# A new order for the first key tile, and the clamp in phi moved to GpSimd

One core of one Trainium2 chip. The metric is device time of one execution in microseconds (us), the median of several runs.

## The reference, cut to what matters

Two branches on the same `x` (2048 rows of 512, bf16), mixed by a gate of each row:

```python
qkv = x @ wqkv                                              # attention branch, 32 heads of 16
phi = lambda t: where(t > 0, t + 1, exp(t)) + 1e-6
kv  = einsum("bhsd,bhse->bhde", phi(k), v); z = sum(phi(k), over s)
o   = (phi(q) @ kv) / (phi(q) . z) ;  a = o @ wo
b   = gelu(layernorm(x).T @ w1 + b1) @ w2 + b2, transposed   # token branch
out = g * a + (1 - g) * b,  g = sigmoid(sum(x * gate_w))
```

phi is computed as max(t, 0) + (min(exp(t), 1) + 1e-6). The clamp of the title is the second bracket. phi runs 32 times on tiles of 128 partitions x 512 columns: 16 of keys, then 16 of queries.

## The kernel before

There are four stages. The *key stage* turns each x tile into keys, phi of the keys, and a 512 x 512 product `gacc` of x and phi(k). The *query stage* runs the first `uacc` matmuls of the token branch between the query matmuls. The rest of the `uacc` matmuls and the output stage (`aps`, `yps`) come last. Each engine runs its own instructions in program order (VectorE before: the copy of tile 2 at 6.24 us, its statistics at 6.58, the clamp at 7.60). In the names, kacc2 stands for the key matmuls of x tile 2, xT for a transposed x tile, e for its exp and pk (pqT for queries) for its phi. The parts that matter:

```python
def phi(dst, acc):                            # acc: PSUM bank of a key or query tile
    e = work.tile([P, SC], BF16, ...)
    nc.scalar.activation(out=e, in_=acc, func=Exp)                       # ScalarE
    nc.vector.tensor_scalar(out=e, in0=e, 1.0, 1e-6, min, add)           # VectorE: the clamp
    nc.vector.scalar_tensor_tensor(out=dst, in0=acc, 0.0, in1=e, max, add)   # VectorE: "combine", S(t)

def ln_step(u):                               # statistics of x tile u for the layer norm
    bn_stats, bn_aggr                                                    # VectorE
    if u % 4 == 3:                            # every fourth tile
        nc.vector.tensor_scalar_add(veps, ...)                           # VectorE
        nc.gpsimd.tensor_tensor(rstd, veps, -0.5, pow)                   # GpSimd
...
transpose_tile(0); transpose_tile(1)          # TensorE, then a copy by VectorE and one by ScalarE
for t in range(2): k_part(t, range(2))        # first two of four key matmuls
transpose_tile(2)
ln_step(0)
for t in range(3):
    k_part(t, rest); k_phi(t)
ln_step(1)
for t in range(3, 16):
    k_part(t); k_phi(t)                       # 4 key matmuls, phi
    if t >= 4: g_tile(t - 4)                  # 4 gacc matmuls of the tile 4 back
    if t >  4: ln_step(t - 3)                 # so rstd falls at t = 6, 10, 14
    if t == 6: load_small()                   # three small loads issued by GpSimd
    if t >= 9: ln_apply(t - 9)                # ScalarE: normalise, needs nmr (VectorE, from rstd)
    if t % 4 == 0 and t >= 8: ln_shift(...)   # VectorE: nmr
```

Tiles from 3 on reach TensorE already transposed, by DMA.

Of the kernel before, what the change touches and what calls it, by code (L numbers as in the profile page):

```python
# [7 lines left out]
ACT = mybir.ActivationFunctionType  # L8
# [7 lines left out]
def kernel(  # L16
# [13 lines left out]
    nc = tc.nc  # L30
    P = nc.NUM_PARTITIONS
# [9 lines left out]
    ND = D // P  # L41
# [25 lines left out]
    def keep(shape, dtype, name):  # L67
        return persist.tile(shape, dtype, name=name, tag=name)

    def bank(name, dtype=FP32):  # L70
        return ps.tile([P, SC], dtype, name=name, tag="bank")

    xs = keep([P, NT, D], BF16, "xs")
    hs = keep([P, NT, D], BF16, "hs")
    xT = keep([P, ND, S], BF16, "xT")
# [17 lines left out]
    ident = keep([P, P], BF16, "ident")  # L93
# [18 lines left out]
    def mm(o, lhsT, rhs, start, stop, **kw):  # L112
        nc.tensor.matmul(o, lhsT=lhsT, rhs=rhs, start=start, stop=stop, **kw)  # L113
# [20 lines left out]
    def load_xT(t0, n):  # L134
# [14 lines left out]
        out=ident[:], in_=ident[:], compare_op=ALU.not_equal, fill=1.0, base=0,  # L149
# [5 lines left out]
        out=maskQ[:], in_=maskH[:].rearrange("p (a m) -> p m a", m=2), op=ALU.max, axis=AX.X  # L155
# [4 lines left out]
        out=xT[:, :, 3 * P : 3 * P + 2],  # L160
        in_=xs[:, 0, 0 : 2 * ND].rearrange("p (k c) -> p k c", k=ND),
# [10 lines left out]
    for c, (j0, nb) in enumerate(w1_chunks):  # L172
        w = wpool.tile([P, NT, FB * P], BF16, name="w1c", tag="wc")
        w1c.append(w)
        for t0 in range(0, NT, 8) if c < 3 else (0,):
            t1 = t0 + 8 if c < 3 else NT
            nc.sync.dma_start(
                out=w[:, t0:t1, : nb * P], in_=w1_view[:, t0:t1, j0 * P : (j0 + nb) * P]
# [15 lines left out]
    def warm_up(n, cols=SC):  # L194
        for _ in range(n):
            mm(wps[:, :cols], warm[:, 0:P], warm[:, :cols], True, True)
# [2 lines left out]
    nc.scalar.activation(out=act_warm[:], in_=ones_f[:], func=ACT.Exp)  # L199
    warm_up(6)  # L200

    def transpose_tile(t):
        pt = bank("pt")
        for k in range(ND):
            mm(pt[:, k * P : (k + 1) * P], xs[:, t, k * P : (k + 1) * P], ident[:], True, True)
        H = ND // 2
        src = pt[:].rearrange("p (k s) -> p k s", k=ND)
        dst = xT[:, :, t * P : (t + 1) * P]
        nc.vector.tensor_copy(out=dst[:, 0:H], in_=src[:, 0:H])  # L209
        nc.scalar.activation(out=dst[:, H:], in_=src[:, H:], func=ACT.Copy)  # L210

    def phi(dst, acc):
        e = work.tile([P, SC], BF16, name="e", tag="e", bufs=6)
        nc.scalar.activation(out=e[:], in_=acc[:], func=ACT.Exp)  # L214
        nc.vector.tensor_scalar(  # L215
            out=e[:], in0=e[:], scalar1=1.0, scalar2=PHI_EPS, op0=ALU.min, op1=ALU.add
        )
        nc.vector.scalar_tensor_tensor(  # L218
            out=dst, in0=acc[:], scalar=0.0, in1=e[:], op0=ALU.max, op1=ALU.add
        )  # L220
# [3 lines left out]
    def k_part(t, ks):  # L224
        if t not in kaccs:
            kaccs[t] = bank("kacc")
        for k in ks:
            mm(
                kaccs[t][:], xT[:, k, t * P : (t + 1) * P], wk_sb[:, k, :],
                k == 0, k == ND - 1,  # L230
            )

    def k_phi(t):
        phi(pk[:, t, :], kaccs.pop(t))
# [32 lines left out]
    def q_block(i):  # L267
        c, j = divmod(i, ND)
        qacc = bank("qacc")
        for k in range(ND):  # L270
            mm(
                qacc[:], wq_sb[:, k, j * P : (j + 1) * P], xT[:, k, c * SC : (c + 1) * SC],
                k == 0, k == ND - 1,
            )
        phi(pqT[:, j, c * SC : (c + 1) * SC], qacc)
# [5 lines left out]
    def ln_step(u):  # L281
        ln_stats(u)
        if u % TPC == TPC - 1:
            ln_rstd(u // TPC)

    HEADS = 3
    transpose_tile(0)
    transpose_tile(1)
    for t in range(2):
        k_part(t, range(2))  # L290
    transpose_tile(2)
    ln_step(0)
    for t in range(HEADS):
        k_part(t, range(2 if t < 2 else 0, ND))
        k_phi(t)
    ln_step(1)
# [159 lines left out]
    for j in range(NB0, NF):  # L456
# [19 lines left out]
        out=gg[:], in0=gth[:], scalar1=0.5, scalar2=0.5, op0=ALU.mult, op1=ALU.add  # L476
    )
    nc.vector.tensor_scalar(
        out=c1[:], in0=gth[:], scalar1=-0.5, scalar2=0.5, op0=ALU.mult, op1=ALU.add
# [3 lines left out]
    for t in range(NT):  # L483
        c, tl = divmod(t, TPC)
        aps = bank("aps")
        for j in range(ND):
# [3 lines left out]
            out=a_sc[:], in_=aps[:], func=ACT.Identity,  # L490
            scale=gg[:, t : t + 1], bias=c2[:, t : t + 1],
        )
        for c0, W in ((0, D - P), (D - P, P)) if t == NT - 1 else ((0, D),):
            cs = slice(c0, c0 + W)
            yps = bank("yps")
            for f in range(NF):
# [6 lines left out]
                out=ot[:, :W], in0=yps[:, :W], scalar=c1[:, t : t + 1], in1=a_sc[:, cs],  # L503
# [35 lines left out]
```

## Time and profile before

| | before |
|---|---|
| median time | 164.42 us (164.37 to 164.69) |
| span of the profiled run | 162.3 us |
| TensorE busy | 157.4 us, 97% of the span |
| GpSimd busy | 17.5 us, 11% |
| first `uacc` matmul (key stage over) | 33.00 us |
| `den` matmuls (query stage and the sum z over) | 71.62 us |

The table is to be read with two marks in mind: everything before 33.00 us is the key stage, and from 71.62 us to the end only TensorE counts. The two marks in the TensorE timeline (start, duration; the other lines stand in the prediction):

```profile
33.00 0.81 PE L113 MATMUL uacc<-hs,w1c 128*128 128x512 bf16 x3
...
71.62 1.06 PE L113 MATMUL denps<-pqT,Z 128*32 128x512 bf16 x16
```

### The profile page before, as it was taken

How to read it: one execution, taken by the hardware profiler on the slowest of the kernel's cores; microseconds unless marked ns; L12 is line 12 of the kernel's file. 1: busy time of each engine (PE TensorE's matmuls, PEld its weight loads, DVE VectorE, ACT ScalarE, POOL GpSimd, SP SyncE). 2: the span in 40 equal slices, each digit the busy share in tenths (PEclk: the TensorE clock that was granted, in tenths of full speed). 3: DMA queues.
4: the chain of work that ended last, by engine and by line, in shares of the span. 5: the costliest groups of instructions: out<-in, count | busy, mean ns of one | idle time of the engine just before them, and what ended most of it. 6: DMA issues, size and time to landing. Idle time of an engine off the chain costs nothing.

```text
span 162.3 us, 2177 instructions
## 1 busy us (share of the span) xinstructions
PE 157.4 (97%) x819; PEld 72.2 (44%) x833; DVE 89.8 (55%) x212; ACT 63.1 (39%) x98; POOL 17.5 (11%) x34
## 2 busy tenths in 40 slices
PE   7899999999999999999999999999999999999993
PEld 2444444444444444444444444444444444444452
DVE  1699999967999999519995301256211111111112
ACT  3552294748677483112865113111122222111110
POOL 3000701200110000001415500050000000000000
DMA  5999999999910007600992699732000001110001
GB/s 156 239 220 231 277 321 325 379 385 386 358 30 0 0 0 233 219 4 0 284 325 88 201 326 313 278 128 71 32 32 32 32 32 42 48 43 33 32 32 32
DMA packets 30569, 25.18 MB, mean 155 GB/s; under 512 B 8480, under 2 KB 29984, under 8 KB 30560
## 3 DMA queue, kind: packets, MB, share of 16 engines
q1 hardware_dynamic: 28288, 21.89, 43.4%
q0 software_dynamic: 1440, 2.38, 5.4%
q10 hardware_dynamic: 832, 0.79, 1.5%
q8 instruction: 6, 0.10, 0.3%
q14 instruction: 3, 0.02, 0.0%
HBM read 21.11 MB, written 2.23 MB: 144 GB/s over the span
## 4 chain that ended last, share of the span: by engine, by line
PE 95%; DMA 2%; issue 1%; DVE 0%; SPq 0%
PE uacc L113 30%; PE yps L113 30%; PE gacc L113 8%; PE aps L113 8%; PE kacc L113 8%; PE qacc L113 8%; DMA xs<-in_A_x_dram 2%; PE denps L113 1%; PE pt L113 0%; PE kvps L113 0%; DVE xT L209 0%; SPq L129 0%; PE w2ps L113 0%; DVE ot L502 0%; PE pt L332 0%
## 5 line engine op out<-in xcount | busy, mean ns | idle before, releaser
L113 PE MATMUL uacc<-hs,w1c 128*128 128x512 bf16 x220 | 51.1, 379 | 0.2
L113 PE MATMUL yps<-uT,w2c 128*128 128x512 bf16 (+2 forms) x234 | 50.6, 366 | 0.2
L502 DVE SCALAR_TENSOR_TENSOR ot<-yps,c,a_sc 128x512 bf16<-128x512 f32 (+2 forms) x17 | 12.2, 719 | 44.7 <-PE yps L113 41.5
L113 PEld LDWEIGHTS <-w2c 128*128 128x128 bf16 x238 | 22.8, 98 | 25.9
L113 PEld LDWEIGHTS <-w1c 128*128 128x128 bf16 x224 | 21.8, 98 | 26.3 <-issue 0.2
L489 ACT ACTIVATE a_sc<-aps,c,gg 128x512 f32<-128x512 f32 x16 | 12.4, 777 | 46.7 <-PE aps L113 39.9
L326 ACT ACTIVATE uT<-uacc,bcol 128x512 bf16<-128x512 f32 x14 | 9.3, 688 | 21.7 <-PE uacc L113 21.7
L113 PE MATMUL qacc<-xT,wq_sb 128*128 128x512 bf16 x61 | 16.1, 379 | 0.2
L113 PE MATMUL aps<-W2sb,pqT 128*128 128x512 bf16 x63 | 16.2, 379 | 0.1
L113 PE MATMUL kacc<-wk_sb,xT 128*128 128x512 bf16 x63 | 16.1, 379 | 0.2
L113 PE MATMUL gacc<-pk,xs 128*128 128x512 bf16 x63 | 15.7, 379 | 0.0
L254 ACT ACTIVATE hs<-xs,nmr,rstd 128x512 bf16<-128x512 bf16 x16 | 12.8, 806 | 3.1 <-DVE nmr L248 3.1
L214 ACT ACTIVATE e<-qacc 128x512 bf16<-128x512 f32 x16 | 9.6, 597 | 9.2 <-PE qacc L113 9.2
L441 POOL DMA_DIRECT2D rex<-rd_dram x16 | 9.4, 601 | 22.5 <-DVE pqT L443 20.0
L214 ACT ACTIVATE e<-kacc 128x512 bf16<-128x512 f32 x16 | 9.3, 593 | 6.6 <-DVE mv L239 2.3
L218 DVE SCALAR_TENSOR_TENSOR pqT<-qacc,e 128x512 bf16<-128x512 f32 x16 | 11.1, 692 | 0.6
L218 DVE SCALAR_TENSOR_TENSOR pk<-kacc,e 128x512 bf16<-128x512 f32 x16 | 11.1, 692 | 0.6
L113 PEld LDWEIGHTS <-xs 128*128 128x128 bf16 x76 | 7.2, 100 | 9.4 <-DMA xs<-in_A_x_dram 1.6
L238 DVE BATCH_NORM_STATS2 stats<-xs 128x6 f32<-128x512 bf16 x16 | 10.9, 684 | 0.0
L215 DVE TENSOR_SCALAR e<-e 128x512 bf16<-128x512 bf16 x32 | 9.0, 281 | 2.3 <-ACT e L214 2.1
L428 DVE CUSTOM_DVE_ANT_0 junk<-xs,gw_b 128x512 bf16<-128x512 bf16 x16 | 9.8, 681 | 0.0
L279 DVE TENSOR_TENSOR zacc<-zacc,pk 128x512 f32<-128x512 f32 x14 | 9.6, 685 | 0.2
(61 smaller groups left out, 70.1 us busy)
## 6 DMA issues: line engine op xcount, KB each, us to landing
w1c<-in_B_w_dram SPq DMA_DIRECT2D x7, 1024.0 KB, 10.7
w2c<-in_B_w_dram SPq DMA_DIRECT2D x8, 896.0 KB, 5.9
rex<-rd_dram POOLq DMA_DIRECT2D x16, 128.0 KB, 4.0
out_dram<-ot SPq DMA_DIRECT2D x13, 128.0 KB, 1.7
xs<-in_A_x_dram SPq DMA_DIRECT2D x3, 512.0 KB, 4.6
wk_sb<-in_A_wqkv_dram ACTq DMA_DIRECT2D x2, 256.0 KB, 3.5
xs<-in_A_x_dram SPq DMA_DIRECT2D x4, 128.0 KB, 3.4
wq_sb<-in_A_wqkv_dram SPq DMA_DIRECT2D x1, 512.0 KB, 6.8
```

The lines of the kernel that those rows point to most:

```text
L113: nc.tensor.matmul(o, lhsT=lhsT, rhs=rhs, start=start, stop=stop, **kw)
L214: nc.scalar.activation(out=e[:], in_=acc[:], func=ACT.Exp)
L215: nc.vector.tensor_scalar(out=e[:], in0=e[:], scalar1=1.0, scalar2=PHI_EPS, op0=ALU.min, op1=ALU.add)
L218: nc.vector.scalar_tensor_tensor(out=dst, in0=acc[:], scalar=0.0, in1=e[:], op0=ALU.max, op1=ALU.add)
L238: nc.vector.bn_stats(out=stats[:], in_=xs[:, t, :])
L254: nc.scalar.activation(out=hs[:, t, :], in_=xs[:, t, :], func=ACT.Identity, scale=rstd[:, t : t + 1], bias=nmr[:, t : t + 1],)
L279: nc.vector.tensor_tensor(out=zacc[:], in0=first, in1=pk[:, t, :], op=ALU.add)
L326: nc.scalar.activation(out=uT[:, j, :], in_=acc[:], func=ACT.Gelu_apprx_tanh, bias=bcol[:, j : j + 1])
L428: nc.vector.tensor_tensor_reduce(out=junk[:], in0=xs[:, t, :], in1=gw_b[:], scale=1.0, scalar=0.0, op0=ALU.mult, op1=ALU.add, accum_out=gp ...
L441: nc.gpsimd.dma_start(out=rex[:], in_=src.unsqueeze(1).to_broadcast([8, HEAD, SC]))
L489: nc.scalar.activation(out=a_sc[:], in_=aps[:], func=ACT.Identity, scale=gg[:, t : t + 1], bias=c2[:, t : t + 1],)
L502: nc.vector.scalar_tensor_tensor(out=ot[:, :W], in0=yps[:, :W], scalar=c1[:, t : t + 1], in1=a_sc[:, cs], op0=ALU.mult, op1=ALU.add,)
```

## The change

The intent: fill the 0.40 us in which TensorE waits for x tile 1 with the first key matmuls of tile 0; let the two copies of a transposed tile run beside each other by giving each a PSUM bank; and take the clamp off VectorE, which is back to back in the key stage, to an engine that is 11% busy.

```diff
-    def transpose_tile(t): one bank, four matmuls, copy of half by VectorE, half by ScalarE
+    def transpose_part(t, k0, k1, on_act): a bank of its own, copied by one engine
+    def transpose_tile(t):
+        transpose_part(t, 0, ND // 2, False)
+        transpose_part(t, ND // 2, ND, True)
     def phi(dst, acc):
-        nc.vector.tensor_scalar(
+        nc.gpsimd.tensor_scalar(
             out=e[:], in0=e[:], scalar1=1.0, scalar2=PHI_EPS, op0=ALU.min, op1=ALU.add
-    transpose_tile(0)
+    transpose_part(0, 0, 1, False)
+    transpose_part(0, 1, 2, False)
+    transpose_part(0, 2, ND, True)
+    k_part(0, range(2))
     transpose_tile(1)
-    for t in range(2):
-        k_part(t, range(2))
+    k_part(1, range(2))
+    k_part(0, range(2, ND))
+    k_phi(0)
     transpose_tile(2)
     ln_step(0)
-    for t in range(HEADS):
+    for t in range(1, HEADS):
```

(The bodies of the transposes are cut to a line.)

More of the change, by code (lines that the diff above doesn't have):

```diff
@@ L200, with transpose_part @@
     warm_up(6)
-    def transpose_tile(t):
-        pt = bank("pt")
-        for k in range(ND):
-            mm(pt[:, k * P : (k + 1) * P], xs[:, t, k * P : (k + 1) * P], ident[:], True, True)
-        H = ND // 2
-        src = pt[:].rearrange("p (k s) -> p k s", k=ND)
-        dst = xT[:, :, t * P : (t + 1) * P]
-        nc.vector.tensor_copy(out=dst[:, 0:H], in_=src[:, 0:H])
-        nc.scalar.activation(out=dst[:, H:], in_=src[:, H:], func=ACT.Copy)
+    def transpose_part(t, k0, k1, on_act):
+        pt = bank("pt")
+        for k in range(k0, k1):
+            mm(pt[:, k * P : (k + 1) * P], xs[:, t, k * P : (k + 1) * P], ident[:], True, True)
+        src = pt[:, k0 * P : k1 * P].rearrange("p (k s) -> p k s", k=k1 - k0)
+        dst = xT[:, k0:k1, t * P : (t + 1) * P]
+        if on_act:
+            nc.scalar.activation(out=dst, in_=src, func=ACT.Copy)
+        else:
+            nc.vector.tensor_copy(out=dst, in_=src)
+    def transpose_tile(t):
+        transpose_part(t, 0, ND // 2, False)
+        transpose_part(t, ND // 2, ND, True)
     def phi(dst, acc):
```

## The prediction

> **What bounds the kernel now.** I read the page first, then the waits, then the timelines of the four compute engines in the key stage (0 to 33 us), then those of GpSimd over the whole run.
>
> ```profile
> PE 157.4 (97%) x819; PEld 72.2 (44%) x833; DVE 89.8 (55%) x212; ACT 63.1 (39%) x98; POOL 17.5 (11%) x34
> PE 95%; DMA 2%; issue 1%; DVE 0%; SPq 0%
> ```
>
> The first line is busy time per engine, the second the chain that ended last. TensorE bounds the kernel and has no slack after its start, so only two things can move the time: idle time of TensorE taken out, or idle time put in. The start is the only place with any to take out. From the TensorE timeline of the first 6.6 us (start, duration):
>
> ```profile
> 3.36 0.63 PE L113 MATMUL pt<-ident,xs 128*128 128x128 bf16 x4
> 4.40 0.40 PE L113 MATMUL pt<-ident,xs 128*128 128x128 bf16 x4 [0.40 <-DMA xs<-in_A_x_dram]
> 4.63 1.29 PE L113 MATMUL kacc<-wk_sb,xT 128*128 128x512 bf16 x4
> 5.80 0.40 PE L113 MATMUL pt<-ident,xs 128*128 128x128 bf16 x4
> ```
>
> TensorE idles 0.40 us for x tile 1; that gap is what the reorder wants to fill. In the key loop it takes 1.73 us a tile (key matmuls of one tile, gacc matmuls of an older one, 0.86 each). How near the helpers are to that pace is in the VectorE and ScalarE timelines between 26 and 38 us:
>
> ```profile
> 26.55 0.68 DVE L238 BATCH_NORM_STATS2 stats<-xs 128x6 f32<-128x512 bf16 x1
> 27.27 0.18 DVE L239 BATCH_NORM_AGGREGATE mv<-stats 128x2 f32<-128x6 f32 x1
> 27.37 0.13 DVE L248 SCALAR_TENSOR_TENSOR nmr<-mv,rstd 128x4 f32<-128x4 f32 x1
> 27.41 0.29 DVE L215 TENSOR_SCALAR e<-e 128x512 bf16<-128x512 bf16 x1
> 27.73 0.69 DVE L218 SCALAR_TENSOR_TENSOR pk<-kacc,e 128x512 bf16<-128x512 f32 x1
> ...
> 31.00 0.17 DVE L243 TENSOR_SCALAR veps<-mv 128x4 f32<-128x4 f32 x1
> 31.08 0.28 DVE L215 TENSOR_SCALAR e<-e 128x512 bf16<-128x512 bf16 x1
> 31.40 0.69 DVE L218 SCALAR_TENSOR_TENSOR pk<-kacc,e 128x512 bf16<-128x512 f32 x1
> ```
>
> ```profile
> 27.53 0.81 ACT L254 ACTIVATE hs<-xs,nmr,rstd 128x512 bf16<-128x512 bf16 x1 [1.71 <-DVE nmr L248]
> 28.25 0.57 ACT L214 ACTIVATE e<-kacc 128x512 bf16<-128x512 f32 x1
> ```
>
> VectorE works back to back: combining max with e (I call it S(t)) to S(t+1) is 1.72 us (27.73 to 29.45), of which the clamp is 0.29. The last, S(15), starts at 31.40 and ends at 32.09; the gacc matmuls of tile 15 start at 32.13, so the key stage already ends just on it. ScalarE does exp 14 only after the normalising of x tile 4, which waits for nmr from VectorE. GpSimd's own timeline:
>
> ```profile
> 16.88 1.04 POOL L244 TENSOR_TENSOR rstd<-veps,mhalf 128x4 f32<-128x4 f32 x1 [14.69 <-DVE veps L243]
> 17.89 0.76 POOL L186 DMA_DIRECT2D brow<-in_B_b_dram  x1
> 18.64 0.55 POOL L187 DMA_DIRECT2D brow<-in_B_b_dram  x1
> 19.18 0.60 POOL L188 DMA_DIRECT2D gw_b<-in_gate_w_dram  x1
> 24.09 1.04 POOL L244 TENSOR_TENSOR rstd<-veps,mhalf 128x4 f32<-128x4 f32 x1 [4.30 <-DVE veps L243]
> 31.25 1.01 POOL L244 TENSOR_TENSOR rstd<-veps,mhalf 128x4 f32<-128x4 f32 x1 [6.12 <-DVE veps L243]
> ```
>
> It looks free, but it is not an empty queue: three times in this stage it stands still until VectorE has made veps, then needs 1.0 us for rstd; the first time three loads (1.9 us) follow. Nobody waits for it now.
>
> **What the skill says.** The Trainium skill's "PSUM — Partial Sum Buffer", Engine vs sequencer instructions, has the ScalarE, VectorE and GpSimdE queues as strict FIFO. The trace agrees: all three run in program order (the copy of tile 2, 6.24, statistics, 6.58, and only then clamp, 7.60). Its "GPSIMD Engine Reference", Elementwise — side-by-side cycle accounting, gives 1.03 cycles an element at 1.2 GHz to a body of at most two operations, so 0.44 us for 512. No such operation is in the trace; its nearest are an affine select of 8 columns at 0.23 us and of 128 at 0.29. I take 0.44 + 0.23 = 0.67, with a little rounding c = 0.70 us (an estimate) for the clamp that VectorE does in 0.28. "SBUF — State Buffer", Who interferes with whom, says that a GpSimd operation that reads SBUF and a VectorE operation with two SBUF inputs exclude each other. In the key loop the large VectorE operations have at most one SBUF input; in the query stage z_add (0.68 us) has two. No run shows the exclusion yet.
>
> **The change, part by part.**
>
> *Start.* Tile 0's copies shrink to 128 columns, so the first key matmul can go when the weights land (issue at 0.80 plus 3.2 us of flight: 4.0). Two go into the 0.40 us gap, but the wait for tile 1's copy (ends 5.27) now has nothing to fill it. After it come kacc1 (2), kacc0 (2), tile 2's transposes (0.23), kacc1 (2), at 0.216 each: TensorE is ready for kacc2 at 5.31 + 6 × 0.216 + 0.23 = 6.84 instead of 6.90. Gain 0.06 us. Separate banks also let the ScalarE copy run beside VectorE's (now 1.2 us waits), off the path.
>
> *New order at tile 2.* phi of tile 0 now stands before tile 2's copy in both queues. kacc0's last matmul starts 5.96, ends 6.34; exp 6.38 to 6.98; clamp 7.02 to 7.72; S(0) at 7.76; the VectorE copy of tile 2 0.61 behind it (the pitch of two such operations), 8.37 to 8.80; kacc2 at 8.84. Against 6.90 that is +1.94, and TensorE has only kacc1's two matmuls to do meanwhile.
>
> *Clamp on GpSimd.* VectorE loses 32 × 0.28 = 9.0 us, off the path. But in GpSimd's queue rstd of tiles t−6 to t−3 stands after clamp t and before clamp t+1 (t = 6, 10, 14), and it waits for statistics that VectorE makes only after S(t). So S(t+1) follows S(t) by: 0.61 (S) + 0.72 (statistics) + 0.22 (aggregate) + 0.25 (veps to rstd) + 1.01 (rstd) + c + 0.04 = 2.85 + c = 3.55; at t = 6 with 1.89 for the loads, 5.44. In between VectorE needs 0.61 + 0.72 + 0.10 = 1.43 a tile. The nmr wait of ScalarE makes a second loop: S(8) to S(10) is 0.61 + 0.72 + 0.10 + 0.16 (nmr) + 0.72 (normalise) + 0.60 (exp) + 0.04 + c + 0.04 = 3.69, and the same from S(12) to S(14).
>
> The working, kacc6 starting 5.19 after kacc2 (6 tiles' worth of 0.86):
> - kacc6 14.03, done 15.06; exp to 15.70; clamp to 16.44; S(6) 16.48
> - S(7) 21.92; S(8) 23.35; S(10) 27.04; S(11) 30.59; S(12) 32.02; S(14) 35.71; S(15) 39.26, done 39.95
> - gacc of tile 15 at 40.00 against 32.13: +7.87 us
>
> Four PSUM banks hide part of it on the way (a tile's bank is wanted again 6.9 us later): kacc11 wants 22.67 and has S(7) done at 22.61; kacc15 wants 29.58 and must wait for S(11), 31.28. Then the gacc matmuls of 13 to 15 wait in turn for their pk. Everything behind starts from the last gacc matmul in the same relation as before. In the query stage GpSimd has one more rstd (t = 4), a lag of about 3.55 − 1.51 = 2.0 us; five banks of 1.51 us hide that, z_add's exclusion too. z_column ends at 67.2 and is wanted at 71.6. So 164.42 + 7.87 = 172.3 us. The 1.94 of tile 2 is inside that sum, not on top.
>
> **The rivals.** *A: all is hidden.* GpSimd is 11% busy and clamp work of 32 × 0.70 = 22 us is a seventh of the span; VectorE is relieved; only the gap at the start counts: about 164.3. Against it: FIFO order makes tile 2's copy late for certain. *B: only tile 2 counts*, the rstd waits being hidden by banks and by the four tiles that gacc lags: 164.42 + 1.94 = 166.4. For it: VectorE gains 0.29 a tile. Against it: four tiles cost 3 × 1.43 + 3.55 = 7.84 us, or 1.43 + 3.69 + 3.55 = 8.67 with the loop over ScalarE, against TensorE's 6.9, and the loads come on top. *C: the clamp is much slower than the estimate.* It enters the path seven times (S(0), 6, 7, 10, 11, 14, 15), so each 0.1 us is worth 0.7 us: c = 1.1 gives 175.1, c = 0.5 gives 170.9. *D: TensorE's clock falls back.* The skill's "TensorE: Matmul & The Clock Gate", What's actually happening, has it halve after an idle window of about 3.4 µs. The trace shows the warm-up (0.43 us a matmul until 3.4 us, 0.216 after). My waits are 1 to 3 us each, so I expect no fall; one would add 1 to 2 us.
>
> **Range and chances.** The order of the queues I hold for nearly certain, the clamp's 0.5 to 1.1 us is the main spread: 170.2 to 174.8. For within 2% (below 167.7) B would have to hold: 0.09. Faster needs more than the start holds: 0.01.
>
> **What would show it.** Right: VectorE's copy of tile 2 near 8.4 instead of 6.24; clamps on GpSimd near 0.7 us; rstd near 18.3, 28.8, 37.4; VectorE idle in the key stage with "e" from GpSimd as what ended it; TensorE waiting for pk at its end; the first uacc matmul near 40.9 instead of 33.00; nothing new after that. Wrong: rstd at the old spacing of 7.2 us (then B), clamps over 1 us (C), matmul spacing of 0.43 us after a wait (D), new TensorE waits in the query stage.

## The result

The changed kernel takes 194.51 us (194.07 to 195.03, 4 runs) against 164.39 (164.21 to 164.69) for the kernel before on the same chip: a ratio of 1.183, 95% interval 1.180 to 1.186. Ratios here are the mean time of one kernel's fast runs over that of the other's in the same rounds, so not quite the ratio of the medians quoted. Executions over 1.5% slower than the fastest of the same kernel are left out of the means. The direction was right, the size was not: the loss is 30.1 us where 7.9 was forecast.

The page of the changed kernel, busy time, and the TensorE clock that was granted in each fortieth of the span (tenths of full speed; the page of before has no such line; its granted clock is on record as 1.000):

```profile
PE 165.6 (86%) x819; PEld 73.5 (38%) x833; DVE 83.6 (43%) x181; ACT 62.6 (32%) x98; POOL 78.9 (41%) x66
...
PEclk9969999978859999999999999999999999999999
...
PE 51%; POOL 31%; DVE 9%; issue 5%; ACT 3%; POOLq 0%; ACTq 0%
```

The third line is the chain that ended last. TensorE holds 51% of it instead of 95; GpSimd, which was on none of it, has 31%. TensorE is busy for 8 us *longer* with the same 819 matmuls, which is the first sign of the clock. The costliest group, from the same page:

```profile
L220 POOL TENSOR_SCALAR e<-e 128x512 bf16<-128x512 bf16 x32 | 61.4, 1918 | 17.3 <-ACT e L219 15.2
```

One clamp takes 1.918 us. VectorE needed 0.281. The prediction had estimated 0.70.

The TensorE timeline of the key stage, cut to where it waits (start, duration; in brackets how long TensorE had stood and what ended it):

```profile
10.20 4.45 PE L113 MATMUL kacc<-wk_sb,xT 128*128 128x512 bf16 x12 [3.10 <-DVE xT L211]
...
29.73 1.02 PE L113 MATMUL kacc<-wk_sb,xT 128*128 128x512 bf16 x4 [3.85 <-DVE pk L223]
...
41.66 1.87 PE L113 MATMUL kacc<-wk_sb,xT 128*128 128x512 bf16 x4 [3.00 <-DVE pk L223]
...
53.56 1.86 PE L113 MATMUL gacc<-pk,xs 128*128 128x512 bf16 x4 [3.84 <-DVE pk L223]
55.22 1.48 PE L113 MATMUL uacc<-hs,w1c 128*128 128x512 bf16 x3
```

Each wait of the key stage is one that the prediction named: tile 2's copy behind the combine of tile 0, a key tile for its PSUM bank, the last gacc groups for their phi. But four matmuls take 1.86 us in places, where they took 1.03 before.

GpSimd's queue in the same stage:

```profile
12.27 9.91 POOL L220 TENSOR_SCALAR e<-e 128x512 bf16<-128x512 bf16 x5 [1.18 <-ACT e L219]
24.00 1.04 POOL L249 TENSOR_TENSOR rstd<-veps,mhalf 128x4 f32<-128x4 f32 x1 [1.83 <-DVE veps L248]
25.02 0.80 POOL L186 DMA_DIRECT2D brow<-in_B_b_dram  x1
25.81 0.55 POOL L187 DMA_DIRECT2D brow<-in_B_b_dram  x1
26.35 0.60 POOL L188 DMA_DIRECT2D gw_b<-in_gate_w_dram  x1
27.02 5.92 POOL L220 TENSOR_SCALAR e<-e 128x512 bf16<-128x512 bf16 x3
```

Five clamps in 9.91 us: a pitch of 2.00 us a tile. Then the queue stands for 1.83 us until VectorE has made veps, spends 1.0 on rstd and 2.0 on the loads, and only then clamps tile 7: 4.8 us without a clamp. The second and third rstd (37.82 and 49.75) repeat the standstill without the loads.

Where the 31.0 us of span went is read from the two marks. The first `uacc` comes at 55.22 instead of 33.00: 22.2 us in the key stage. The `den` matmuls come at 102.62 instead of 71.62: 8.8 more in the query stage. From there to the end both kernels take 90.7 us. The waits in the query stage are new; three of the eight that are listed there (all together 5.7 us):

```profile
74.75 1.02 PE L113 MATMUL qacc<-xT,wq_sb 128*128 128x512 bf16 x4 [1.89 <-DVE pqT L223]
...
86.98 13.97 PE L113 MATMUL uacc<-hs,w1c 128*128 128x512 bf16 x63 [0.97 <-DVE pqT L223]
...
102.62 1.05 PE L113 MATMUL denps<-pqT,Z 128*32 128x512 bf16 x16 [1.07 <-DVE Z L375]
```

### The profile page after: what moved, and what is told of

Same layout as the page of the kernel before. It is cut to its first block, busy times and chain, and to the rows that moved or that the text cites. A ratio compares the mean times of both kernels' runs of the same rounds, so it can differ in the third digit from the quotient of the medians.

```text
span 193.3 us, 2197 instructions
## 1 busy us (share of the span) xinstructions
PE 165.6 (86%) x819; PEld 73.5 (38%) x833; DVE 83.6 (43%) x181; ACT 62.6 (32%) x98; POOL 78.9 (41%) x66
## 4 chain that ended last, share of the span: by engine, by line
PE 51%; POOL 31%; DVE 9%; issue 5%; ACT 3%; POOLq 0%; ACTq 0%
POOL e L220 28%; PE yps L113 25%; PE uacc L113 13%; PE aps L113 7%; POOL rstd L249 2%; DVE zacc L284 2%; ACT e L219 2%; PE kacc L113 2%; DVE pk L223 1%; PE wps L113 1%; DVE pqT L223 1%; PE gacc L113 1%; DVE stats L243 1%; ACT hs L259 1%; PE qacc L113 1%
## 5 line engine op out<-in xcount | busy, mean ns | idle before, releaser
L220 POOL TENSOR_SCALAR e<-e 128x512 bf16<-128x512 bf16 x32 | 61.4, 1918 | 17.3 <-ACT e L219 15.2
L113 PE MATMUL uacc<-hs,w1c 128*128 128x512 bf16 x220 | 51.9, 383 | 1.2 <-DVE pqT L223 1.0
L511 DVE SCALAR_TENSOR_TENSOR ot<-yps,c,a_sc 128x512 bf16<-128x512 f32 (+2 forms) x17 | 12.2, 720 | 44.8 <-PE yps L113 41.6
L113 PE MATMUL kacc<-wk_sb,xT 128*128 128x512 bf16 x63 | 18.9, 426 | 11.9 <-DVE pk L223 8.0
L113 PE MATMUL gacc<-pk,xs 128*128 128x512 bf16 x63 | 17.5, 409 | 5.7 <-DVE pk L223 5.7
L113 PE MATMUL qacc<-xT,wq_sb 128*128 128x512 bf16 x61 | 16.8, 391 | 4.0 <-DVE pqT L223 3.7
L113 PEld LDWEIGHTS <-xT 128*128 128x128 bf16 x64 | 6.5, 105 | 21.9 <-issue 12.6
L113 PEld LDWEIGHTS <-xs 128*128 128x128 bf16 x76 | 7.7, 105 | 15.8 <-issue 8.9
L113 PEld LDWEIGHTS <-wq_sb 128*128 128x128 bf16 x64 | 6.4, 100 | 12.9 <-issue 6.5
```

Source lines behind the costliest of these rows:

```text
L113: nc.tensor.matmul(o, lhsT=lhsT, rhs=rhs, start=start, stop=stop, **kw)
L220: nc.gpsimd.tensor_scalar(out=e[:], in0=e[:], scalar1=1.0, scalar2=PHI_EPS, op0=ALU.min, op1=ALU.add)
L511: nc.vector.scalar_tensor_tensor(out=ot[:, :W], in0=yps[:, :W], scalar=c1[:, t : t + 1], in1=a_sc[:, cs], op0=ALU.mult, op1=ALU.add,)
```

## The experiments

Twelve kernels. "Before" is run beside each; its medians lay between 164.1 and 164.4.

### What the operation costs: e1_probe

Nine kinds of GpSimd operation, three times each, on dead tiles in the output stage of the kernel before, where GpSimd is empty:

```diff
+    g.tensor_scalar(out=hs[:, 0, :], in0=x0, min 1.0, add 1e-6)            # line 490
+    the same on 256 columns (491), on 128 (492); min alone (493); f32 (494);
+    mult 1.0, add 1e-6 (495); copy (496); add of two tiles (497); mult alone (498)
```

> The kernel before, with nine kinds of GpSimd operation added three times each on dead tiles in the last stage, where GpSimd is otherwise empty; the results are thrown away. It measures the term that the prediction took as 0.70 us and that the changed kernel shows as 1.92. Theory 1 (the cost is per element, some 3.6 ns each, for both operations together): 512 columns 1.9 us, 256 columns 1.0, 128 columns 0.55; the form with one operation and the copy clearly below 1.9. Theory 2 (a large fixed cost of this instruction): 128 columns still above 1.2 us. Theory 3 (it was lengthened in the changed kernel by VectorE working beside it): here, with VectorE nearly idle, 512 columns fall to 0.7 to 1.2 us. The time of the kernel stays at 164.4 in all three.

Time 164.54 (one run; before 164.43). The groups of GpSimd (busy, mean ns of one):

```profile
L490 POOL TENSOR_SCALAR hs<-xs 128x512 bf16<-128x512 bf16 x3 | 5.8, 1939 | 0.2
L494 POOL TENSOR_SCALAR zT<-zacc 128x512 f32<-128x512 f32 x3 | 5.8, 1924 | 0.2
L498 POOL TENSOR_SCALAR hs<-xs 128x512 bf16<-128x512 bf16 x3 | 4.5, 1503 | 0.0
L493 POOL TENSOR_SCALAR hs<-xs 128x512 bf16<-128x512 bf16 x3 | 4.5, 1489 | 0.2
...
L497 POOL TENSOR_TENSOR hs<-xs 128x512 bf16<-128x512 bf16 x3 | 3.5, 1153 | 0.0
L491 POOL TENSOR_SCALAR hs<-xs 128x256 bf16<-128x256 bf16 x3 | 3.2, 1066 | 0.2
L492 POOL TENSOR_SCALAR hs<-xs 128x128 bf16<-128x128 bf16 x3 | 2.1, 686 | 0.2
L495 POOL TENSOR_SCALAR hs<-xs 128x512 bf16<-128x512 bf16 x3 | 1.9, 621 | 0.2
L496 POOL COPY hs<-xs 128x512 bf16<-128x512 bf16 x3 | 1.8, 611 | 0.2
```

Theory 1 holds: from 256 to 512 columns the clamp grows by 0.87 us, 3.4 ns a column, with about 0.2 us fixed (128 columns took 0.69, where 0.55 was expected). Theories 2 and 3 fall: it is as slow with VectorE nearly idle, and in f32. What was not expected is how much the *form* matters: min with add 1.94, min alone 1.49, mult alone 1.50, but mult with add 0.62, no more than a copy. The prediction's sum of 0.67 comes near that one form and is wrong by a factor of 2.9 for the one in the kernel. Why the forms differ no run shows.

### The start alone: e2_start_only

```diff
-        nc.gpsimd.tensor_scalar(          # of the changed kernel
+        nc.vector.tensor_scalar(
```

> The new start and order, the clamp back on VectorE. My theory (the order at tile 2 puts exp, clamp and combine of tile 0 ahead of tile 2's copy, whatever engine clamps): exp 0 ends 7.08, clamp 0.29, combine at 7.4, copy of tile 2 at 8.0, kacc2 at 8.45 instead of 6.90: plus 1.5 us, 166.0. Rival (the start as the change meant it: the gap is filled): 164.0 to 164.4.

Measured 165.73 (ratio 1.008, 1.006 to 1.011): the start by itself costs 1.3 us. kacc2 starts at 8.64 after a wait of 1.42 for tile 2's copy; before it was 6.90. So the order at tile 2 loses with the clamp on VectorE too, as theory had it.

### The clamp alone: e3_clamp_only

```diff
-        nc.vector.tensor_scalar(          # of the kernel before
+        nc.gpsimd.tensor_scalar(
```

> The start and order of before, only the clamp on GpSimd. My theory (from the first clamp on GpSimd's queue is the path, so the order at tile 2 is paid by nobody a second time): first clamp at 7.6 instead of 7.17, but no wait of 1.2 us for exp 2: 7 clamps end at 21.6 instead of 22.2, so about 0.6 us off: 193.9. Rival (the stall at tile 2, 3.3 us of TensorE, is paid in the end): 194.5 less 3 us, 191.5.

Measured 194.20 (193.75 to 194.57; ratio 1.181, 1.178 to 1.185): the 0.3 us that the old start saves of 30 is within the noise. The new order at tile 2 costs almost nothing once GpSimd is the path, because what TensorE loses at the start it would later lose waiting for a clamp: with the old start it waits 4.90 us for the bank of a key tile (until 29.31), with the new one 3.85 (until 29.73). Nearly all of the result is the clamp.

### The queue with nothing but clamps: e4_empty_queue

```diff
-        nc.gpsimd.tensor_tensor(out=rstd[:, s], in0=veps[:, s], in1=mhalf[:], op=ALU.pow)
+        nc.vector.tensor_scalar(out=rstd[:, s], in0=veps[:, s], scalar1=-4000.0, scalar2=30.0,
+                                op0=ALU.mult, op1=ALU.add)     # a line through the expected variance
-        nc.gpsimd.dma_start(out=brow ...)                     # and the two others
+        nc.scalar.dma_start(out=brow ...)
```

> The changed kernel with rstd taken off GpSimd (a straight line through the expected variance on VectorE, a slightly wrong result on purpose) and the three small loads issued by ScalarE, so that GpSimd's queue holds clamps alone. My theory (sum of a pitch of 2.00 us a tile, which is over TensorE's 1.73 and 1.51, and of the rstd waits): 16 clamps end near 40.3 instead of 52.8, the last gacc near 41 instead of 53.6 (12.4 us off), the query stage 3 us shorter: 179. Rival A (the rstd waits and loads are nearly the whole loss): 166 to 169. Rival B (the pitch alone is the loss, waits hidden): 192 or more.

Measured 180.84 (179.61 to 182.21; ratio 1.100). So 13.7 of the 30.1 us are GpSimd's standstills for rstd and its loads, with what they do to TensorE's clock, and 16.4 remain with clamps alone in the queue. Both rivals fall. The last gacc group starts at 42.99 (expected 41): ScalarE still does exps 10 and 14 behind a normalise that waits for nmr.

### The forecast's own size: e5_fast_form

```diff
-            out=e[:], in0=e[:], scalar1=1.0, scalar2=PHI_EPS, op0=ALU.min, op1=ALU.add
+            out=e[:], in0=e[:], scalar1=1.0, scalar2=PHI_EPS, op0=ALU.mult, op1=ALU.add
```

> The changed kernel with min replaced by mult in the GpSimd operation (times 1.0, plus the small constant: no clamp, a wrong result on purpose). The probe has this form at 0.62 us for 512 columns where min and add take 1.94, so the duration comes to lie where the prediction put it (0.70), with every queue order kept. If only the size of the clamp was wrong in the prediction, its sum gives 172.3 less 7 times 0.08: 171.7, with tile 2's copy near 8.3, the first uacc near 40.3 and no waits of TensorE in the query stage. Rival (the prediction's rstd chain was wrong too, the banks hide it): 166.4 or less.

Measured 174.72 (173.54 to 175.36; ratio 1.062), 3.0 over the expectation; it happens that the comparison with the reference lets the missing clamp pass. This run has the prediction's clamp (0.62 for 0.70) with every queue as in the changed kernel, so it shows which steps were right. The combine of tile t starts, in us:

| step | predicted, c = 0.70 | fast form, c = 0.62 | one op, c = 1.49 | changed kernel, c = 1.92 |
|---|---|---|---|---|
| S(6) | 16.48 | 17.01 | 20.53 | 22.20 |
| to S(7): rstd and loads | 5.44 | 5.46 | 6.33 | 6.78 |
| S(7) to S(8) | 1.43 | 1.43 | 1.45 | 2.00 |
| S(8) to S(10): nmr | 3.69 | 3.71 | 4.61 | 5.05 |
| to S(11): rstd | 3.55 | 3.58 | 4.35 | 4.88 |
| S(11) to S(12) | 1.43 | 1.42 | 1.45 | 2.00 |
| S(12) to S(14): nmr | 3.69 | 3.71 | 4.61 | 5.04 |
| to S(15): rstd | 3.55 | 3.54 | 4.34 | 4.86 |

The steps of the chain agree within 0.03 us although c is 0.08 less, so each of the five with a wait was worked out some 0.1 us too short, 0.5 in all; and each of the five grows with c about one to one. The rest of the miss is at the two ends (the profiled run took 175.36, so 3.7 over). At the start TensorE was still at half pace when the two key matmuls of the gap came:

```profile
4.19 1.01 PE L113 MATMUL kacc<-wk_sb,xT 128*128 128x512 bf16 x2
...
40.61 1.86 PE L113 MATMUL gacc<-pk,xs 128*128 128x512 bf16 x4 [2.52 <-DVE pk L223]
42.27 1.49 PE L113 MATMUL uacc<-hs,w1c 128*128 128x512 bf16 x3
```

Two matmuls take 1.01 us there (0.38 apart; in the start-alone run 0.59 us, 0.21 apart), though the granted clock is on record as 1.00 in that stretch. They also start 0.19 later than forecast, and kacc2 comes at 9.42, 0.7 after the 8.76 that the sum gives for this c. And at the end the granted clock falls to 0.50: the last gacc group and the first tiles of the query stage take nearly twice as long. From that group to the first exp of a query (45.50) it is 4.9 us against 2.58 before: 2.3 us. After that TensorE has no wait in the query stage: with this c the prediction's "nothing new after that" holds, but for the clock.

### One operation in place of two: e6_one_op

```diff
-            out=e[:], in0=e[:], scalar1=1.0, scalar2=PHI_EPS, op0=ALU.min, op1=ALU.add
+            out=e[:], in0=e[:], scalar1=1.0, scalar2=None, op0=ALU.min
```

> The changed kernel with the clamp as min alone, without the second operation (the constant added is 1e-6 and is lost in bf16 beside most values, so the result should pass). The probe has it at 1.49 us: a pitch of 1.57 a tile, under TensorE's 1.73 in the key stage, a little over 1.51 in the query stage. My theory (the prediction's chain with the true size): S(0) 8.6, kacc2 9.6, S(6) 19.2, S(7) 25.5, S(10) 31.5, S(11) 35.9, S(14) 42, S(15) 46.3, so the last gacc near 47 against 32.1; the query stage ends hidden; with 1 to 2 us of halved clock 180 to 182. Rival (only the pitch against TensorE's pace counts; 1.57 is under 1.73, so the key stage is hidden): 166 to 169.

Measured 182.44 (181.17 to 183.92, the last run slow; the three fast ones have the median 182.41; ratio 1.106), result correct, 0.4 us over the expectation. Its pitch, 1.45 us, is under TensorE's 1.73, so by throughput alone the key stage would have been hidden; S(15) comes at 47.67 all the same (expected 46.3). The chain of waits, not the pace, is what counts in this stage.

### Keys alone, queries alone: e7_keys_only, e8_queries_only

```diff
+    def phi(dst, acc, eng): ... eng.tensor_scalar(...)   # e7: keys GpSimd, queries VectorE; new start
+                                                        # e8: keys VectorE, queries GpSimd; old start
```

> The changed kernel with the clamp of the queries back on VectorE, that of the keys on GpSimd. My theory (key stage 22.2 us of the 30, query stage and what hangs on it 8.8): the first uacc still near 55.2, no waits of TensorE after that: 186. Rival (the two stages share one loss, GpSimd being late once): 192 or more, or 175 and less.

Measured 188.00 (187.31 to 188.37; ratio 1.143). First `uacc` at 55.27 as expected; no wait of TensorE for phi after it. 2 us over the expectation: the key stage alone brings a loss of 23.6 with the halved clock behind it.

> The kernel before, with the clamp of the queries alone on GpSimd. My theory: the first clamp at 35.3, 16 of them at 2.00 with the rstd wait of 3 us inside, last combine 71.0, then six sums and the column of z 7.7 us: the den matmuls at 78.7 instead of 71.6, so plus 7.1: 171.5. The key stage is untouched (first uacc 33.0). Rival (the banks hide the query stage, as the prediction had it): 164.4 to 166.

Measured 171.88 (171.39 to 172.08; ratio 1.045); `den` at 78.98, expected 78.7. The query stage alone loses 7.5 us, and the banks do not hide it: what counts there is not a wait of TensorE on the way but that the last clamp ends 68.64 + 1.93 = 70.57, and six sums for z and the column of z stand behind it. The two losses make 31.2 together, the full change 30.1, so they add up but for 1 us.

### The clock: e9_filler

```diff
+    fill = bank("uacc")                      # later the first of the three uacc banks
     for t in range(NT - LAG, NT):
+        if t == NT - 1:
+            for _ in range(18):
+                mm(fill[:], warm[:, 0:P], warm[:], True, True)
         g_tile(t)
```

> The changed kernel with 18 dummy matmuls on constants, results overwritten later, put between the gacc groups of tiles 14 and 15, where TensorE waits 3.84 us for the clamp of tile 15. They keep TensorE busy in that wait without touching GpSimd. My theory: the halved clock (0.50 in the records from 52 to 58 us of the changed kernel) costs 2.3 us there (from the last gacc group to the first exp of a query 4.9 us against 2.58 in the kernel before): with the filler 192.2, and a clock of 1.0 in that stretch. Rival (the halved clock costs nothing, as GpSimd is the path anyway): 194.5, or more if the filler delays the last group.

Measured 192.83 (192.54 to 194.31; ratio 1.176, 1.172 to 1.180, against 1.183, 1.180 to 1.186, of the changed kernel): 1.7 us better by the medians and 1.2 by the ratios, whose intervals meet at 1.180, where 2.3 was expected. By windows of 2 us (columns: window, its length, busy time of the five engines, granted clock, DMA share, GB/s), first the changed kernel, then the filled one:

```profile
54.00:56.00 2.00, 2.00 (x6) 0.68 (x5) 1.56 (x5) 1.19 (x2) 0.00 (x0) 0.50 0.01 4
56.00:58.00 2.00, 1.78 (x5) 0.73 (x5) 0.15 (x1) 0.00 (x0) 0.00 (x0) 0.50 0.00 0
```

```profile
54.00:56.00 2.00, 2.00 (x11) 0.94 (x10) 1.36 (x4) 0.93 (x3) 0.00 (x0) 1.00 0.01 4
56.00:58.00 2.00, 2.00 (x12) 0.94 (x11) 0.00 (x0) 1.03 (x3) 1.33 (x1) 1.00 0.00 0
```

Useless matmuls in the wait keep the clock at 1.00, and twice as many matmuls pass in the 4 us behind it (the count in the first bracket). From the last group to the first exp of a query it is now 53.35 to 55.92, 2.57 us, as before. So the halved clock at this place is real in the trace and is worth 1 to 2 us of time; it is not the bulk.

### What is left of the change: e10_start_mended, e11_start_stats

```diff
     k_part(0, range(2, ND))                  # of the changed kernel, clamp on VectorE
-    k_phi(0)
     transpose_tile(2)
+    k_phi(0)                                 # e10: here
     ln_step(0)
+    k_phi(0)                                 # e11: here instead
```

> What is left of the change when both losses are taken out: the new start with separate banks, clamp on VectorE, and phi of tile 0 placed behind tile 2's transposes instead of ahead of them. My theory: kacc2 at 6.84 to 6.9 as in the kernel before, a gain of at most 0.1 us: 164.3 to 164.4. Rival (filling the gap of 0.40 us is worth its whole length): 164.0.

Measured 165.28 (164.79 to 165.33; ratio 1.005, 1.003 to 1.008): 0.9 us slower than before by the ratio where a gain of up to 0.1 was expected. That expectation is wrong. Its chain through the key stage is VectorE's, down to the last combine at 32.61, and TensorE waits 0.65 us for the last phi (last gacc group at 33.35). The statistics of tile 0 (0.9 us), which the kernel before does in VectorE's idle time ahead of the first exp, had come behind the first combine.

> The mended start with one more order put back: the statistics of x tile 0 ahead of phi of tile 0, as in the kernel before. In the run with the mended start VectorE was the chain through the whole key stage (0.65 us of TensorE waiting at its end), because 0.9 us of statistics had left the idle time that VectorE had ahead of the first exp. My theory (that shift is the whole of its 0.9 us): last combine ends near 32.1 again, first uacc at 33.0 to 33.2, 164.1 to 164.4, same as before. Rival (the extra VectorE copy, or separate banks, cost it): 164.8 to 165.3 as without.

Measured 164.48 (164.13 to 165.05; ratio 1.001, 0.997 to 1.005): the same as before. With both orders put right, filling the gap is worth nothing that can be measured, since kacc2 is no earlier (6.73 plus two matmuls of tile 1, so 7.16, for 6.90) and the first `uacc` comes at 33.33 for 33.00. No version beat the kernel before.

### Both terms taken away: e12_fast_empty

The fast form of e5 with the emptied queue of e4.

> The changed kernel with both taken away: the fast form of the operation (times 1.0 and add, 0.62 us, no clamp, wrong on purpose) and GpSimd's queue emptied of rstd and loads. If the fast-form run's 10 us come from the waits in that queue and what they do to the clock, what is left is the order at tile 2 with 0.62 in place of 0.29: kacc2 at 8.3 to 9.4 instead of 6.9, so plus 1.4 to 2.5: 165.8 to 167, and no stretch of halved clock after the start. Rival (some 8 us belong to something else in moving the operation to GpSimd, such as its semaphores): over 170.

Measured 166.53 (166.09 to 166.72; ratio 1.012), with the clock full after the start and no wait of TensorE longer than the 1.80 us for tile 2's copy. From 174.72 to 166.53 is 8.2 us: what GpSimd's queue holds besides the clamps is worth that much even with a fast operation. Of the 2.3 us that are left, the start by itself cost 1.3 (start-alone run): the move to another engine as such costs hardly anything once the operation is short and the queue is empty.

## Why the prediction was right or wrong

**The bound and where time could go in** were right: TensorE had no slack, and every wait that it now has in the key stage is at a place that the prediction named; those in the query stage it had ruled out.

**The order at tile 2** was right. The clamp-free part of it shows in the start-alone run (kacc2 at 8.64), and it was right that its 1.94 us are not on top of the chain: with the old start 194.20, with the new 194.51, no difference clear of noise.

**The rstd chain** was right in structure and, for its own c, within about 0.1 us a step (the table above). That rival B would not hold is shown by the one-op run, whose pitch fits under TensorE's and which still loses 18 us.

**The clamp, c = 0.70 us, is the term that failed**: it measured 1.918. The second step that failed hangs on it: that the banks hide the query stage. The prediction took the 1.03 cycles an element of the Trainium skill ("GPSIMD Engine Reference", Elementwise — side-by-side cycle accounting) and added the fixed cost of another operation; this form takes 3.4 ns an element where 1.03 cycles at 1.2 GHz are 0.86. The prediction knew that c enters seven times and that it had no measurement of it, and yet kept the top of its spread at 1.1. (Two slips in its sums are small beside this: its range ends at 174.8 though its own 1.1 gives 175.1, and begins at 170.2 though its 0.5 gives 170.9; and the third rstd comes at 37.5 by its chain, not 37.4.) Its rule of 0.7 us for each 0.1 would have given 172.3 + 12.2 × 0.7 = 180.8 for the true c, so more than the size went wrong. With c = 1.92 the pitch of GpSimd, 2.00, is over VectorE's 1.43 and TensorE's 1.73 and 1.51, and the sum loses its form:

- S(6) was to be paced by TensorE; it stands behind five clamps in a row instead (from 12.27): 22.20 for 16.48, so 5.7 us.
- S(6) to S(15) takes 30.61 for 22.78: 7.8 us, of which five steps with waits give 6.7 and the two plain ones 1.1.
- The last gacc group takes 1.66 us for 0.86, by the clock: 0.8. The three make 14.3 of the 14.4 by which the first `uacc` missed its 40.86.
- "Nothing new after that" failed: the query stage lost 8.8. A lag of 2.0 us that five banks hide was worked out with a pitch under 1.51; at 2.00 a tile, sixteen tiles and one rstd wait run past the end of the stage, and z behind them. 1.5 of the 8.8 is clock (55.22 to the first exp 58.45, against 33.00 to 34.71). With c = 0.62, in the fast-form run, the stage was hidden.

**Rival D, the clock,** was put aside because no wait would reach 3.4 us. In the changed kernel it fell back behind waits of 3.10, 3.00 and 3.84 us, and not behind one of 3.85 (the four matmuls at 29.73 take 1.02 us); in the fast-form run it fell back behind 1.25 and 2.52 with one group between. In the emptied queue the last gacc group took 1.87 us after waits of 0.98, 1.90 and 1.07 with work between them, while a wait of 3.11 for tile 2's copy left the clock full there (12 key matmuls in 2.76 us; in the changed kernel 4.45 after the wait of 3.10). So the length of one wait does not decide it; what does, no run shows. With the clamp at about its forecast size this rival was worth 2.3 us (fast-form run, 174.72), so the point of 172.3 would have missed by about as much even then.

**The start** was half right: it gains nothing that can be measured, but for one reason more than was given. The prediction counted 0.216 us a key matmul in the gap; in six of the ten runs with the new start (one trace of each) the two took 0.95 to 1.03 us together (0.60 in the others at full pace), since TensorE was still at the slow pace of the warm-up at about 4.1 us. The prediction let the warm-up end at 3.4 us; its own lines show four transposes still taking 0.63 us at 3.36 and 0.40 at 4.40.

## What to carry to other kernels

Before an operation is moved to an engine for which the trace has no such operation, measure that very form beside the old kernel on dead data; a neighbouring form can be three times faster. Then write down that engine's whole queue in program order: an idle engine whose queue waits for the engine that it is to relieve closes a loop, and each trip round it that no buffer hides is paid, however low its busy share. And a chain of small waits costs more than their sum when TensorE's clock falls back behind them.

## What the Trainium skill lacked or had wrong

- "GPSIMD Engine Reference", Elementwise — side-by-side cycle accounting: 1.03 cycles an element at k ≤ 2 (that k counts operations is the prediction's reading) gives 0.44 us for 512 columns. Mult with add (0.62 us) and copy (0.61) fit it if some 0.18 us are fixed, which was not measured; min with add (1.94), min alone (1.49) and mult alone (1.50) do not. The page has no table of forms.
- "TensorE: Matmul & The Clock Gate", What's actually happening: the row on the idle state gives one idle window of about 3.4 µs. Read as the length of one wait, that does not fit; the page says more of the clock further on, which was not tested here. Here it was halved behind waits of at most 1.90 us with matmuls in between (four matmuls in 1.87 us instead of 1.03), it was full behind single waits of 3.11 and 3.85 us, and 18 dummy matmuls in a wait of 3.84 us kept it up.
- "SBUF — State Buffer", Who interferes with whom: a VectorE operation with two SBUF inputs contends with a GpSimd operation that reads SBUF, and the lock on the shared port pair is exclusive. In the query stage of the changed kernel z_add runs wholly inside a clamp, for instance from 80.86 to 81.54 within one from 80.30 to 82.22, at its usual length of 0.68 us (median of 14: 0.682 in both kernels; one took 0.84). No full exclusion shows, only some operations drawn out: in the fast-form run one z_add took 0.99 and one clamp 0.74 where 0.62 is usual. Whether one delays the start of the other stays open: in the fast-form run one wait of a clamp, 0.57 us, is put down to z_add.
